# Attention memory into a feed-forward layer: eight small products side by side for scores and folds, heads ordered by even and odd, and three of the small accumulators moved to the first product's banks

## The chip, the core and the metric

The program runs on one core of one Trainium2 chip. A core has TensorE (matrix products, written to the accumulator memory PSUM, which has eight banks of 2 KB for each of its 128 partitions), VectorE (DVE in the profile), ScalarE (ACT), GpSimd (POOL) and SyncE (SP, which only issues DMAs here). The profile shows TensorE in two rows: PE, the products, and PEld, the loading of the stationary operand. The metric is the device time of one execution in microseconds (us).

## The reference

For each of 8 batches and 8 heads there are 576 tokens, a head width of 64 and 32 memory slots. What is computed, cut to what matters:

```python
a = exp(phi - max(phi, tokens)); a = a / sum(a, tokens)      # (b, h, s, 32)
k_m, v_m = a.T @ k, a.T @ v                                  # (b, h, 32, 64)
scores = q @ k_m.T / 8;  attn = softmax(scores, slots)       # (b, h, s, 32)
x = attn @ v_m                                               # tokens x 512
h = x @ w_in;  g = h * cos(h);  out = g @ w_out              # 512 -> 2048 -> 512
```

There are 4608 tokens in all. The inputs are float32, the two weights float64.

## The kernel before, in words

The product `attn @ v_m @ w_in` is regrouped: for each batch the 8 x 32 memory slots are multiplied into `w_in` once (the "fold", 256 x 2048), and the tokens are then multiplied with the folded weight. So the first large product has a contraction of 256 (two chunks of 128, index g) in place of 512.

**The main loop** (from line 660) has 192 steps: 12 groups of 384 tokens by 16 slices of the inner width. A step takes the first product of its slice (`gemm1`, line 493, into one of three banks of the pool ps_h), the cosine (`act`, `act_end`, lines 502 to 519: ACT, two DVE operations, ACT, DVE, ACT, DVE, after the fifth of which the bank is free), and the second product of a slice some five steps earlier (`gemm2`, line 537, into three banks of the pool ps_acc). From the second group on, float16 parts take the place of float32: a step has six products of 384 columns (or twelve of 192, where a group spans two batches) and nine of 512. A pair of batches takes 48 steps.

**The preparation of a batch** (`prep`, a generator: `memory`, line 214, then `attend`, line 324) is threaded into the steps before its first use. The job list (line 645) gives each batch its stretch of steps; the loop advances the generator so that it would reach 24 resumptions at the end of the stretch (NSTEP, lines 641 and 688). In order the resumptions hold: the maximum of phi spread over the partitions ("top", a product with the identity for the first four batches; a GpSimd reduction, `maximum`, line 204, from the fifth on); subtraction and Exp; the memory sums psA, one token chunk of 128 for each resumption, five in all, the last of 64 tokens (line 247: eight products of 32 columns a chunk, four side by side in the four 32-column strips); the loads of the next batch and the division (X, line 261); the transposition tpx (line 267) into km and vm (lines 274 to 277), which are zeroed first and hold a pair of heads as a block-diagonal 128 x 64; a bound on v for its scale (lines 281 to 287); the scores in three blocks of 256, 256 and 64 tokens (line 349: four products of 128 rows by 64 columns, two side by side, into one bank, then one DVE transposition, line 351); then the softmax and its split into two float16 parts.

**The fold** (lines 421 to 445) is placed by a second list (line 649): for each batch four quarters of the inner width (index q), two halves each (index g), a half every second step. From the third batch on a half is eight products in `fold_psum`: the high part vp of v_m against four strips, then its low part vl, which is padded with zeros in the rows of the other part of `w_in`, against the same four strips. Each product takes 128 rows, 32 columns and 512 columns of weights (line 432). ACT and DVE then split the bank into two float16 parts (lines 438 and 439).

**Banks.** Three pools share the eight banks: ps_acc has three, ps_h three (lines 51 and 52), and ps_s two (line 53), from which top, psA, tpx, each block of scores and each half of a fold take one.

**Order.** The kernel's framework gives each engine a fixed order of instructions when the program is built. It starts from the order of the code, but puts later work ahead of an instruction whose bank or operand its own estimates call not ready; only instructions that are pinned (`tc.keep_in_program_order`) stay. At run time each engine works through its own list, with semaphores for the rest.

## Time and profile before

| | |
|---|---|
| median of 3 runs | 719.82 us (718.49 to 720.54) |
| the profiled execution | 718.65 us, of which its span is 716.6 us |
| mean granted TensorE clock | 0.990 |
| PE busy | 694.8 us, 97% of the span |
| DVE busy | 570.0 us, 80% |
| ACT busy | 520.8 us, 73% |
| POOL busy | 14.1 us, 2% |

A row of the timeline has the start, the time from the first start to the last end, the engine, the line, the operation, the tiles (out<-in), the shapes and the count. Products overlap: one of 512 columns shows 0.38 us, but the next one starts 0.216 us after it. A float32 product is two rows, one for each of its passes. "128\*32" is the part of the array that a product takes: rows by columns.

### The profile page before, as it was taken

Reading aid. Unit: us, or ns where it says so; the run is one execution under the profiler, and the core shown is the slowest. Engines: PE = TensorE matmul, PEld = TensorE weight load, DVE = VectorE, ACT = ScalarE, POOL = GpSimd, SP = SyncE. Lnnn points to the kernel's source line nnn. Section 1 sums busy time; section 2 is a strip of 40 time slices with the busy share of each in tenths; the row PEclk is TensorE's granted clock in tenths of the full one; section 3 lists DMA queues with packets and bytes.
Section 4 is the critical chain, followed back from the end, with each engine's and each line's share of the span. In section 5 each row is a group of like instructions: output and inputs, shape, how many; then the busy total and the mean of one; then the engine's idle time right before and its main releaser. Section 6 shows DMA issues by size and latency. Waiting matters only on the chain.

```text
span 716.6 us, 12018 instructions
## 1 busy us (share of the span) xinstructions
PE 694.8 (97%) x4578; PEld 357.2 (50%) x4578; DVE 570.0 (80%) x1256; ACT 520.8 (73%) x965; POOL 14.1 (2%) x34
## 2 busy tenths in 40 slices
PE   7689999999999999999999999999999999999997
PEld 3244444565454445565444544666444544555553
DVE  2868999998988997679877997679776987676753
ACT  1789999899886875668757685678767785665653
POOL 0000000000000000000000100000000000000000
PEclk9799999999999999999999999999999999999999
DMA  8995881426405300152103310152100000100101
GB/s 291 381 330 168 310 291 42 121 60 188 149 7 161 111 1 1 45 167 67 45 1 123 107 49 1 45 167 68 44 1 1 22 24 1 45 1 1 45 0 45
DMA packets 31561, 66.78 MB, mean 93 GB/s; under 512 B 2192, under 2 KB 11024, under 8 KB 31504
## 3 DMA queue, kind: packets, MB, share of 16 engines
q1 hardware_dynamic: 27184, 58.15, 25.1%
q10 hardware_dynamic: 4320, 7.87, 2.9%
q8 instruction: 36, 0.59, 0.3%
q14 instruction: 21, 0.17, 0.1%
HBM read 52.38 MB, written 9.44 MB: 86 GB/s over the span
## 4 chain that ended last, share of the span: by engine, by line
PE 60%; ACT 17%; DVE 16%; DMA 4%; issue 2%; SPq 1%; POOL 0%; ACTq 0%; DVEq 0%
PE acc L537 34%; PE hp L493 18%; PE pv L432 3%; ACT u L512 2%; DVE u L516 2%; DMA phi<-in_phi 2%; DVE u L508 2%; DVE gp L519 2%; ACT u L502 2%; ACT L512 2%; DVE gp L507 1%; DMA kv<-in_kv 1%; PE sc L349 1%; ACT L237 1%; PE psA L247 1%
## 5 line engine op out<-in xcount | busy, mean ns | idle before, releaser
L537 PE MATMUL acc<-wo,gp 128*128 128x512 f16 x1584 | 371.2, 379 | 0.0
L537 PEld LDWEIGHTS <-gp 128*128 128x128 f16 x1584 | 153.4, 98 | 161.5 <-issue 2.6
L493 PE MATMUL hp<-aT,vw 128*128 128x192 f16 (+1 forms) x1440 | 202.6, 284 | 0.8 <-DVE u L516 0.4
L493 PEld LDWEIGHTS <-vw 128*128 128x128 f16 x1440 | 125.1, 98 | 82.3 <-issue 30.0
L512 ACT ACTIVATE u<-u 128x384 f32<-128x384 f32 x192 | 99.7, 522 | 86.6 <-DVE u L508 85.7
L516 DVE SCALAR_TENSOR_TENSOR u<-hp,u 128x384 f32<-128x384 f32 x176 | 96.8, 552 | 45.7 <-ACT u L512 43.4
L502 ACT ACTIVATE u<-hp,cu 128x192 f32<-128x192 f32 (+1 forms) x240 | 110.3, 491 | 18.2 <-PE hp L493 11.8
L519 DVE TENSOR_TENSOR gp<-u,gp 128x384 f16<-128x384 f32 x176 | 96.6, 551 | 29.9 <-ACT gp L518 29.3
L518 ACT CAST gp<-u 128x384 f16<-128x384 f32 x176 | 89.0, 509 | 38.7 <-DVE u L516 36.7
L508 DVE TENSOR_TENSOR u<-u,gp 128x384 f32<-128x384 f32 x192 | 105.7, 552 | 3.2
L507 DVE CAST gp<-u 128x384 int32<-128x384 f32 x192 | 67.4, 353 | 20.6 <-ACT u L502 18.9
L532 PE MATMUL acc<-wo,gp 128*128 128x512 f32 x96 | 45.5, 603 | 1.6 <-DVE gp L514 1.6
L439 DVE SCALAR_TENSOR_TENSOR vw<-pv,vw 128x512 f16<-128x512 f32 x48 | 33.0, 689 | 5.1 <-ACT vw L438 3.8
L438 ACT ACTIVATE vw<-pv 128x512 f16<-128x512 f32 x48 | 28.3, 590 | 7.4 <-PE pv L432 6.5
L484 PE MATMUL hp<-aT,vf 128*128 128x384 f32 x64 | 26.4, 546 | 4.2 <-DVE gp L514 2.0
L512 ACT ACT_TABLE_LOAD x23 | 29.5, 1283 | 0.4
L532 PEld LDWEIGHTS acc<-wo,gp 128*128 128x128 f32 x96 | 17.0, 190 | 20.7 <-issue 14.9
L247 PE MATMUL psA<-kv,phi 128*32 128x129 f32 (+1 forms) x640 | 23.5, 276 | 2.8 <-DMA kv<-in_kv 1.5
L553 ACT ACTIVATE ob<-acc,os 128x512 f32<-128x512 f32 x28 | 18.5, 682 | 8.1 <-PE acc L537 5.2
L247 PEld LDWEIGHTS psA<-kv,phi 128*32 128x32 f32 (+1 forms) x640 | 16.1, 109 | 13.3 <-issue 6.9
L484 PEld LDWEIGHTS hp<-aT,vf 128*128 128x128 f32 x64 | 12.5, 207 | 17.7 <-DVE gp L514 4.6
L349 PE MATMUL sc<-q,km 128*64 128x256 f32 (+3 forms) x192 | 20.6, 343 | 0.0
(126 smaller groups left out, 549.5 us busy)
## 6 DMA issues: line engine op xcount, KB each, us to landing
kv<-in_kv SPq DMA_DIRECT2D x32, 516.0 KB, 5.8
q<-in_qT SPq DMA_DIRECT2D x8, 1152.0 KB, 6.4
raw_out<-in_w_out SPq DMA_DIRECT2D x8, 1024.0 KB, 5.0
out<-ob ACTq DMA_DIRECT2D x30, 256.0 KB, 2.1
raw_in<-in_w_in SPq DMA_DIRECT2D x6, 1024.0 KB, 8.4
phi<-in_phi SPq DMA_DIRECT2D x8, 512.0 KB, 7.2
w_in_sb<-w_in_parts SPq DMA_DIRECT2D x12, 256.0 KB, 4.1
phiT<-in_phiT SPq DMA_DIRECT2D x4, 576.0 KB, 6.4
```

Source lines behind the costliest of these rows:

```text
L247: nc.tensor.matmul(psA[32 * j:32 * (j + 1), g * KV:(g + 1) * KV], lhsT=a[:n, c, h * M:(h + 1) * M], rhs=kvs[c][:n, h * KV:(h + 1) * KV], s ...
L484: nc.tensor.matmul(hp[:, :GT], lhsT=st["vf", q][:, g, fo * P:(fo + 1) * P], rhs=st["aTf"][:, g], start=(g == 0), stop=(g == 1))
L493: nc.tensor.matmul(hp[:, c0:c0 + n], lhsT=vw[:, wi, g, fo * P:(fo + 1) * P], rhs=aT[:, ai, g, c1:c1 + n], start=(k == 0), stop=(k == 5))
L502: ins = nc.scalar.activation(u[:, c0:c0 + n], hp[:, c0:c0 + n], AF.Copy, scale=st["cu", b] if grp else 1.0 / (2.0 * math.pi), bias=0.25)
L507: nc.vector.tensor_copy(out=ni, in_=u)
L508: nc.vector.tensor_tensor(out=u, in0=u, in1=ni, op=ALU.subtract)
L512: nc.scalar.activation(u, u, AF.Sin, scale=TWO_PI_BELOW)
L516: nc.vector.scalar_tensor_tensor(out=u, in0=hp[:, :GT], scalar=2.0 ** -17, in1=u, op0=ALU.mult, op1=ALU.mult)
L518: nc.scalar.copy(gp[:, 0], u)
L519: nc.vector.tensor_tensor(out=gp[:, 1], in0=u, in1=gp[:, 0], op=ALU.subtract)
L532: nc.tensor.matmul(accs[grp][t], lhsT=gp[:, t * P:(t + 1) * P], rhs=wo[:, f + 1], start=(f == 0), stop=(f == NF - 1))
L537: nc.tensor.matmul(accs[grp][t], lhsT=gp[:, gi, t * P:(t + 1) * P], rhs=parts[:, wi], start=(f == 0 and gi == 0 and wi == 0), stop=(f == N ...
```

## The change

For the third batch and those behind it (b >= 2; the first two stay as they are):

- The host puts the even heads ahead of the odd ones, and lays k ahead of v for the even, v ahead of k for the odd. After the transposition, k of the even heads and v of the odd stand in partitions 0 to 63, k of the odd and v of the even in partitions 64 to 127, without zeros between. km, vm and vl lose their padding, and GpSimd's two memsets and the mask of the bound on v fall away.
- A block of scores is eight products of 64 rows by 32 columns in place of four of 128 by 64. The even heads go to one bank, the odd to another, and each bank has a transposition of its own.
- A quarter of a fold is taken at once, into two banks: eight products of 128 by 32 with the high part, then eight of 64 by 32 with the low part. The call for the second half does nothing.
- top, psA and tpx take their bank from ps_h. The pool ps_s is left to scores and folds, which take both of its banks at a time.
- The five chunks of psA are issued without a resumption between them; the generator has four resumptions less, and what stands behind psA comes up to three steps earlier.

```diff
--- before.py
+++ after.py
@@ -58,6 +58,12 @@
     ident = const.tile([P, P], F32, name="ident")
     nc.sync.dma_start(out=ident, in_=eye)
 
+    HALF = (slice(0, D), slice(D, P))
     vmask = const.tile([P, 2, 2], F32, name="vmask")
     nc.vector.memset(vmask, 0.0)
     for j in range(4):
@@ -70,8 +76,11 @@
     def wo_parts(f):
         return wo[:, f].bitcast(F16).rearrange("p (w e) -> p w e", w=2)
 
-    vl = const.tile([P, NP, 2, M], F16, name="vl")
-    nc.vector.memset(vl, 0.0)
+    vl = const.tile([P, NP, M], F16, name="vl")
+    def one_ps(b, name):
+        return small_ps(name) if b < 2 else ps_h.tile([P, 512], F32, tag="ps_h", name=name)
 
     loads, st = {}, {}
 
@@ -217,7 +226,7 @@
 
             nmx = wk.tile([P, 2], F32, tag="nmx", name=f"nmx_{b}", bufs=1)
             nc.vector.tensor_reduce(out=nmx, in_=loads.pop(("phiT", b)), op=ALU.max, axis=AX.X)
-            top = small_ps(f"top_{b}")[:, 0:HM]
+            top = one_ps(b, f"top_{b}")[:, 0:HM]
             for g in range(2):
                 nc.tensor.matmul(top[:, g * P:(g + 1) * P], lhsT=nmx[:, g:g + 1].broadcast_to([P, P]), rhs=ident,
                                  start=True, stop=True)
@@ -239,7 +248,7 @@
         if b:
             yield
         kvs = loads.pop(("kv", b))
-        psA = small_ps(f"psA_{b}")
+        psA = one_ps(b, f"psA_{b}")
         for c, (s0, n) in enumerate(TCH):
             for g in range(2):
                 for j in range(4):
@@ -248,7 +257,8 @@
                         psA[32 * j:32 * (j + 1), g * KV:(g + 1) * KV],
                         lhsT=a[:n, c, h * M:(h + 1) * M], rhs=kvs[c][:n, h * KV:(h + 1) * KV],
                         start=(c == 0 and g == 0), stop=(c == 4), skip_group_check=True)
-            yield
+            if b < 2 or c == 4:
+                yield
         if b >= 1 and b + 1 < B and b + 1 != 2:
             load_phi(b + 1)
             load_kv(b + 1)
@@ -262,25 +272,39 @@
                                     op0=ALU.mult)
         if b:
             yield
-        tpx = small_ps(f"tpx_{b}")
+        tpx = one_ps(b, f"tpx_{b}")
         for g in range(2):
             nc.tensor.matmul(tpx[:, g * P:(g + 1) * P], lhsT=X[:, g], rhs=ident, start=True, stop=True)
-        km = wk.tile([P, NP, 2 * M], F32, tag="km", name=f"km_{b}", bufs=1)
-        vm = wk.tile([P, NP, 2 * M], F32, tag="vm", name=f"vm_{b}")
-        nc.gpsimd.memset(km, 0.0)
-        nc.gpsimd.memset(vm, 0.0)
-        tv = tpx[:, 0:HM].rearrange("p (c t m) -> p c t m", t=2, m=M)
-        lo, hi = slice(0, D), slice(D, P)
-        nc.scalar.mul(km[lo, :, 0:M], tv[lo, :, 0], 1.0 / math.sqrt(D))
-        nc.scalar.mul(km[hi, :, M:2 * M], tv[hi, :, 1], 1.0 / math.sqrt(D))
-        nc.vector.tensor_copy(out=vm[hi, :, 0:M], in_=tv[hi, :, 0])
-        nc.vector.tensor_copy(out=vm[lo, :, M:2 * M], in_=tv[lo, :, 1])
+        n = 2 * M if b < 2 else M
+        km = wk.tile([P, NP, n], F32, tag="km", name=f"km_{b}", bufs=1)
+        vm = wk.tile([P, NP, n], F32, tag="vm", name=f"vm_{b}")
+        if b < 2:
+            nc.gpsimd.memset(km, 0.0)
+            nc.gpsimd.memset(vm, 0.0)
+        lo, hi = HALF
+        if b < 2:
+            tv = tpx[:, 0:HM].rearrange("p (c t m) -> p c t m", t=2, m=M)
+            nc.scalar.mul(km[lo, :, 0:M], tv[lo, :, 0], 1.0 / math.sqrt(D))
+            nc.scalar.mul(km[hi, :, M:2 * M], tv[hi, :, 1], 1.0 / math.sqrt(D))
+            nc.vector.tensor_copy(out=vm[hi, :, 0:M], in_=tv[hi, :, 0])
+            nc.vector.tensor_copy(out=vm[lo, :, M:2 * M], in_=tv[lo, :, 1])
+        else:
+            tv = tpx[:, 0:HM].rearrange("p (g j m) -> p g j m", g=2, m=M)
+            for g in range(2):
+                nc.scalar.mul(km[HALF[g]], tv[HALF[g], g], 1.0 / math.sqrt(D))
+                nc.vector.tensor_copy(out=vm[HALF[1 - g]], in_=tv[HALF[1 - g], g])
         st["km", b], st["vm", b] = km, vm
         yield
-        l1 = wk.tile([P, 4], F32, tag="l1", name=f"l1_{b}")
-        nc.vector.tensor_reduce(out=l1, in_=X.rearrange("p g (t d) -> p (g t) d", t=2), op=ALU.add, axis=AX.X,
-                                apply_absolute_value=True)
-        nc.vector.tensor_tensor(out=l1, in0=l1, in1=vmask.rearrange("p g t -> p (g t)"), op=ALU.mult)
+        if b < 2:
+            l1 = wk.tile([P, 4], F32, tag="l1", name=f"l1_{b}")
+            nc.vector.tensor_reduce(out=l1, in_=X.rearrange("p g (t d) -> p (g t) d", t=2), op=ALU.add, axis=AX.X,
+                                    apply_absolute_value=True)
+            nc.vector.tensor_tensor(out=l1, in0=l1, in1=vmask.rearrange("p g t -> p (g t)"), op=ALU.mult)
+        else:
+            l1 = wk.tile([P, 2], F32, tag="l1", name=f"l1_{b}")
+            nc.vector.tensor_reduce(out=l1, in_=X.rearrange("p g x -> p (g x)")[:, D:3 * D].rearrange(
+                "p (t d) -> p t d", t=2), op=ALU.add, axis=AX.X, apply_absolute_value=True)
         l2 = wk.tile([P, 1], F32, tag="l2", name=f"l2_{b}")
         nc.vector.tensor_reduce(out=l2, in_=l1, op=ALU.max, axis=AX.X)
         l3 = wk.tile([P, 1], F32, tag="l3", name=f"l3_{b}")
@@ -312,10 +336,10 @@
             vp = wk.tile([P, NP, 2, M], F16, tag="vp", name=f"vp_{b}", bufs=1)
             for o in range(2):
                 here, there = slice(o * D, (o + 1) * D), slice((1 - o) * D, (2 - o) * D)
-                vm = st["vm", b][here, :, (1 - o) * M:(2 - o) * M]
+                vm = st["vm", b][here]
                 nc.scalar.activation(vp[here, :, o], vm, AF.Copy, scale=sv[here])
                 nc.scalar.activation(vp[there, :, o], vm, AF.Copy, scale=sv[here])
-                nc.vector.scalar_tensor_tensor(out=vl[here, :, o], in0=vm, scalar=sv[here], in1=vp[here, :, o],
+                nc.vector.scalar_tensor_tensor(out=vl[here], in0=vm, scalar=sv[here], in1=vp[here, :, o],
                                                op0=ALU.mult, op1=ALU.subtract)
             st["vp", b] = vp
 
@@ -343,6 +367,15 @@
 
         def scores(i):
             t0, n = BL[i]
+            if b >= 2:
+                sc = [small_ps(f"sc_{b}_{t0}_{g}") for g in range(2)]
+                for j in range(4):
+                    for g in range(2):
+                        nc.tensor.matmul(sc[g][M * j:M * (j + 1), :n], lhsT=km[HALF[g], j],
+                                         rhs=qt[HALF[g], j, t0:t0 + n], start=True, stop=True)
+                for g in range(2):
+                    nc.vector.transpose(at[:, 2 * t0 + g * n:2 * t0 + (g + 1) * n], sc[g][:, :n])
+                return
             sc = small_ps(f"sc_{b}_{t0}")
             for g in range(2):
                 for p in range(2):
@@ -418,19 +451,25 @@
         yield
 
 
-    def fold_psum(b, q, g):
-        pv = small_ps(f"pv_{b}_{q}_{g}")
+    def fold_32(q, g):
+        pv = small_ps(f"pv_1_{q}_{g}")
         for i in range(2):
             c = 2 * g + i
-            if b < 2:
-                nc.tensor.matmul(pv[D * i:D * (i + 1)], lhsT=st["vm", b][:, c],
-                                 rhs=w_in_sb[:, c, q * FS:(q + 1) * FS], start=True, stop=True)
-        if b >= 2:
-            for first in (True, False):
-                for j in range(4):
-                    c, o = 2 * g + j // 2, 1 - j % 2
-                    nc.tensor.matmul(pv[M * j:M * (j + 1)], lhsT=(st["vp", b] if first else vl)[:, c, o],
-                                     rhs=st["w2", q][:, c, o], start=first, stop=not first, skip_group_check=True)
+            nc.tensor.matmul(pv[D * i:D * (i + 1)], lhsT=st["vm", 1][:, c], rhs=w_in_sb[:, c, q * FS:(q + 1) * FS],
+                             start=True, stop=True)
+        return pv
+    def fold_16(b, q):
+        pv, w2 = [small_ps(f"pv_{b}_{q}_{g}") for g in range(2)], st["w2", q]
+        for g in range(2):
+            for j in range(4):
+                nc.tensor.matmul(pv[g][M * j:M * (j + 1)], lhsT=st["vp", b][:, j, 1 - g], rhs=w2[:, j, 1 - g],
+                                 start=True, stop=False, skip_group_check=True)
+        for j in range(4):
+            for g in range(2):
+                v = HALF[1 - g]
+                nc.tensor.matmul(pv[g][M * j:M * (j + 1)], lhsT=vl[v, j], rhs=w2[v, j, 1 - g],
+                                 start=False, stop=True, skip_group_check=True)
         return pv
 
     def split_fold(b, vw, g, src):
@@ -442,7 +481,11 @@
     def fold(b, q, g):
         if g == 0:
             st["vw", b, q] = wk.tile([P, 2, 2, FS], F16, tag="vw", name=f"vw_{b}_{q}", bufs=8)
-        split_fold(b, st["vw", b, q], g, fold_psum(b, q, g))
+        if b == 1:
+            split_fold(b, st["vw", b, q], g, fold_32(q, g))
+        elif g == 0:
+            for x, pv in enumerate(fold_16(b, q)):
+                split_fold(b, st["vw", b, q], x, pv)
 
     def fold_first(j):
         q, r = divmod(j, 2)
@@ -711,10 +754,16 @@
 
     q, k, v, phi = (np.asarray(inputs[n]) for n in ("q", "k", "v", "phi"))
     w_in, w_out = np.asarray(inputs["moe_w_in"]), np.asarray(inputs["moe_w_out"])
+    k, v, phi = k.copy(), v.copy(), phi.copy()
+    order = list(range(0, H, 2)) + list(range(1, H, 2))
+    for a in (k, v, phi):
+        a[2:] = a[2:, order]
     kv = np.ones((B, S, H, KV), k.dtype)
     kt, vt = k.transpose(0, 2, 1, 3), v.transpose(0, 2, 1, 3)
-    kv[:, :, 0::2, 0:D], kv[:, :, 0::2, D:2 * D] = kt[:, :, 0::2], vt[:, :, 0::2]
-    kv[:, :, 1::2, 0:D], kv[:, :, 1::2, D:2 * D] = vt[:, :, 1::2], kt[:, :, 1::2]
+    for bs, even, odd in ((slice(0, 2), slice(0, H, 2), slice(1, H, 2)), (slice(2, B), slice(0, 4), slice(4, H))):
+        kv[bs, :, even, 0:D], kv[bs, :, even, D:2 * D] = kt[bs, :, even], vt[bs, :, even]
+        kv[bs, :, odd, 0:D], kv[bs, :, odd, D:2 * D] = vt[bs, :, odd], kt[bs, :, odd]
     laid = {
         "phi": np.ascontiguousarray(phi.transpose(0, 2, 1, 3)).reshape(B, S, HM),
         "phiT": np.ascontiguousarray(phi[:NT].transpose(0, 1, 3, 2)).reshape(NT, HM, S),
```

## The prediction

> **What bounds the kernel now.** I read the page first, then the busy time by stretches, the waits of PE, and the chain that ended last; then single visits of PE to the small products.
>
> ```profile
> span 716.6 us, 12018 instructions
> PE 694.8 (97%) x4578; PEld 357.2 (50%) x4578; DVE 570.0 (80%) x1256; ACT 520.8 (73%) x965; POOL 14.1 (2%) x34
> ```
>
> The page says PE, but 97% is an average. The stretches and the waits of PE behind 218 us say where it is true:
>
> ```profile
> 160.00:218.00 58.00, 57.23 (x427) 29.85 (x426) 49.80 (x115) 51.10 (x87) 0.97 (x3) 1.00 0.40 123
> 218.00:640.00 422.00, 420.67 (x2983) 217.84 (x2983) 340.44 (x771) 298.69 (x582) 9.54 (x16) 1.00 0.16 53
> ```
>
> ```profile
> PE pv L432 <- ACT vp L317: 0.4, 1, 0.4
> PE psA L247 <- ACT phi L237: 0.4, 2, 0.2
> PE hp L493 <- DVE u L516: 0.3, 1, 0.3
> ```
>
> The columns of the first are the stretch, its length, and the busy time of PE, PEld, DVE, ACT and POOL, then the granted clock (1.00) and DMA. From 218 to 640 us, where five of the six changed batches have their scores and nearly all of their folds, PE is busy 420.7 of 422 us and waits 1.1 us in all. Time taken off PE there should come off the end. There are two exceptions. Before 218 us, in the preparation of the third batch, DVE (49.8 of 58) and ACT (51.1) are as full as PE, and the chain runs over them. And the chain leaves PE twice later, for some 42 us each (302 to 344, and alike 465 to 507):
>
> ```profile
> 310.50 7.29 DMA phi<-in_phi
> 317.82 0.69 DVE mx L207
> ...
> 343.58 0.48 DVE u L516
> ```
>
> There PE has work, but the work of DVE and ACT is just as late: PE's lists are full only because second products are put ahead while banks of the first are missing. What PE saves in those two stretches counts only if that chain gets shorter too.
>
> **The folds.** A visit to one half of a fold, with the products of 512 columns ahead and those of the next step behind:
>
> ```profile
> 373.94 2.11 PE L537 MATMUL acc<-wo,gp 128*128 128x512 f16 x9
> 375.98 0.40 PE L432 MATMUL pv<-w_in_sb,vp 128*32 128x512 f16 x4
> 376.20 0.39 PE L432 MATMUL pv<-w_in_sb,vl 128*32 128x512 f16 x4
> 376.52 1.15 PE L493 MATMUL hp<-aT,vw 128*128 128x384 f16 x6
> ```
>
> Nine products of 0.216 us bring 373.94 to 375.88; the fold starts 0.10 later, its second round 0.22 after the first, and the next product 0.32 after that, which is a round and 0.10 more. So the visit costs 376.52 - 373.94 - 1.94 = 0.64 us: two rounds of four products side by side, and a switch of the array's shape of 0.10 on each side. There are 48 such visits, 30.7 us; seven lie directly beside psA or scores (one is seen below, at 383.15) and share a switch, 0.2 each, so 29.3 us.
>
> What a switch inside a visit costs is seen in psA, whose last chunk has 64 rows. Two chunks of one shape, and then two of which the second is the one of 64 rows (this view runs them together):
>
> ```profile
> 211.88 0.81 PE L537 MATMUL acc<-wo,gp 128*128 128x512 f16 x3
> 212.62 1.09 PE L247 MATMUL psA<-kv,phi 128*32 128x129 f32 x32
> 213.65 0.82 PE L493 MATMUL hp<-aT,vw 128*128 128x384 f16 x4
> ```
>
> ```profile
> 308.65 0.59 PE L537 MATMUL acc<-wo,gp 128*128 128x512 f16 x2
> 309.18 1.22 PE L247 MATMUL psA<-kv,phi 128*32 128x129 f32 x32
> 310.33 0.50 PE L493 MATMUL hp<-aT,vw 128*128 128x192 f16 x4
> ```
>
> The first visit costs 213.65 - 211.88 - 0.65 = 1.12 us, the second 310.33 - 308.65 - 0.43 = 1.25, so the inner switch is 0.13.
>
> After the change a quarter is one visit: switch 0.10, two rounds for the high parts 0.44, inner switch 0.13, the low parts, and 0.10. If the eight products of 64 by 32 run side by side they are one round, 0.22: together 0.99 us, where two halves cost 1.28. Twenty-four quarters cost 23.8 us; the saving is 5.5 us. No row shows two products in different halves of the rows at once, so this has two bounds: one round or two. I take one, since strips beside each other do run at once (four products in 0.40 us), and the two halves write different banks.
>
> **The scores.** A block of 256 and a block of 64 tokens:
>
> ```profile
> 319.80 0.59 PE L537 MATMUL acc<-wo,gp 128*128 128x512 f16 x2
> 320.33 1.08 PE L349 MATMUL sc<-q,km 128*64 128x256 f32 x8
> 321.35 1.16 PE L493 MATMUL hp<-aT,vw 128*128 128x192 f16 x12
> ```
>
> ```profile
> 327.26 1.24 PE L537 MATMUL acc<-wo,gp 128*128 128x512 f16 x5
> 328.44 0.45 PE L349 MATMUL sc<-q,km 128*64 128x64 f32 x8
> 328.82 0.59 PE L493 MATMUL hp<-aT,vw 128*128 128x192 f16 x5
> ```
>
> The first costs 321.35 - 319.80 - 0.43 = 1.12 us (eight rows, two at a time: four rounds of 0.216, and switches), the second 328.82 - 327.26 - 1.08 = 0.48. A batch costs 2.72, six 16.3, less 0.8 where two blocks share a visit: 15.5 us. Eight at a time leave two of the four rounds: 1.12 - 0.43 = 0.69, and for the small block half of its 0.28 between the switches, so 0.34. Six batches cost 10.3 us; the saving is 5.2. The same doubt holds as for the folds.
>
> **The memory sums.** psA keeps its products, but its five chunks become one visit. Today they lie in two to four:
>
> ```profile
> 380.64 1.46 PE L537 MATMUL acc<-wo,gp 128*128 128x512 f16 x6
> 382.03 0.65 PE L247 MATMUL psA<-kv,phi 128*32 128x129 f32 x16
> 382.61 0.60 PE L537 MATMUL acc<-wo,gp 128*128 128x512 f16 x2
> 383.15 0.40 PE L432 MATMUL pv<-w_in_sb,vp 128*32 128x512 f16 x4
> 383.37 0.39 PE L432 MATMUL pv<-w_in_sb,vl 128*32 128x512 f16 x4
> 383.59 0.61 PE L247 MATMUL psA<-kv,phi 128*32 128x129 f32 x16
> ```
>
> One chunk alone costs 382.61 - 380.64 - 1.30 = 0.67, a further one 1.12 - 0.67 = 0.45. A batch in three visits costs 0.67 + 1.12 + 1.25 = 3.04; six, as they lie, 18.1 us. One visit is 1.25 + 3 x 0.45 = 2.6, six 15.6: a saving of 2.5 us. PE then stands for 2.6 us at one stretch without a first product; DVE and ACT have at that point several slices of cosine to work off, so it costs nothing, unless they have not, where it costs at most those 2.6 us for a batch.
>
> **Other engines and the loads.** DVE's rows:
>
> ```profile
> L351 DVE STREAM_TRANSPOSE at<-sc 128x512 f32<-128x512 f32 x15 | 10.6, 707 | 0.9 <-PE sc L349 0.9
> L372 DVE STREAM_TRANSPOSE aT<-at 128x256 f32<-128x256 f32 x2 | 0.8, 424 | 0.0
> L351 DVE STREAM_TRANSPOSE at<-sc 128x128 f32<-128x128 f32 x7 | 2.1, 305 | 0.0
> L439 DVE SCALAR_TENSOR_TENSOR vw<-pv,vw 128x512 f16<-128x512 f32 x48 | 33.0, 689 | 5.1 <-ACT vw L438 3.8
> ```
>
> A block's transposition of 0.71 us becomes two of 0.42, that of the small block (0.31) two of at most 0.31: 0.6 us more a batch at most, less the mask and half of the reduction that fall away. DVE has 82 us to spare from 218 to 640, so it is off the path except in the two stretches above. GpSimd's memsets go; nobody waited for them. The loads of the next batch's phi, kv and q move with the generator, up to three steps ahead, in SP's queue; only loads stand behind them there. phi has one buffer, so its load starts when psA has been read through. With psA in one visit this comes sooner, which helps the 7.29 us of the chain above.
>
> **New waits.** Each of the 24 quarters and 18 blocks needs both banks of ps_s at once, where today one is filled while the other is read. From below this costs nothing: the order puts other products between. From above it costs the full reading time, two DVE passes: 2 x 0.42 = 0.84 us for a block, 2 x 0.69 = 1.38 for a quarter, 48 us in all. I take 1.0 us in all, near the lower end, since PE's present waits for banks (0.3) show that the planned order fits the chip. top, psA and tpx now hold one of the three banks of the first product: between nothing and the 2.6 us above for a batch; I take 0.5 in all.
>
> **Sum.** PE saves 5.5 + 5.2 + 2.5 = 13.2 us. Off it come the third batch's scores and memory sums and part of the fourth's sums, before 218 us (1.6), half of what the fifth and seventh batches save in the two stretches that DVE and ACT set (2.2, so 1.1), and the new waits (1.5). That leaves 9.0: 718.65 - 9.0 = 709.6 us for an execution like the profiled one. The median of the runs shown is 1.2 above it; I add a part of that: **710.0 us**.
>
> **The rivals.**
>
> *Row halves do not run side by side* (the change then doesn't do what it says). A quarter costs 0.99 + 0.22 = 1.21, twenty-four 29.0: 0.3 saved. Scores cost 16.3 in separate visits: 0.8 lost. psA's 2.5 stay. With the losses of the sum PE gains about 1: 717.5 us, no difference that can be told (0.3%, or 2.2 us, is about what a measurement of this kernel can tell from none). Against it speaks only what strips do. The Trainium skill, TensorEngine Tiling (Array Packing), under Tiling Modes, lists 64 by 32 as eight independent tiles that load and multiply in parallel. By that rule the savings of 5.5 and 5.2 stand; no row here shows such a pair. Chance 0.11.
>
> *DVE and ACT become the bound in the preparations.* DVE is 81% busy from 218 to 640, and the attention parts now lie in fewer, faster steps, with two halves of a fold (1.38 us of DVE) falling in one step of about 2.9 us. Then what is saved inside the preparations is lost, and only the folds outside them count: about two thirds of 5.5, and 1 of psA, 4.5 in all: 714 us. For it speak the two stretches; against it that DVE recovers between them. The Trainium skill, same page, under Performance Considerations (PSUM Bottleneck), warns that tiling speeds up TensorE but not the reading of PSUM. The trace bears this out only in the stretches named. Chance 0.14.
>
> *Slower: PE stands before the two banks of ps_s.* A block of scores that follows a quarter or another block must wait until DVE has read both banks; in the sixth and eighth batches the step lists put a quarter and a block in one step and two blocks in the next. If all 18 blocks wait 0.84 and a quarter of the folds' reading (0.25 of 1.38 for 24) shows as well, that is 15 + 8 = 23 us, less 10.5 saved: 731 us. It decides from 0.27 us a user (42 of them, 11.2 us: the saving and 0.3%). Against it speaks that PE's list has second products ready at nearly every point. Chance 0.09.
>
> **How the numbers follow.** The forecast has 0.66. With the second rival a gain has 0.80, no difference 0.11, slower 0.09. The range reaches from 703.5, where all 13.2 us count and the chain shortens a little, to 717.5, into the first rival; what lies outside is the last rival, half of the first, and little below.
>
> **What would show it.** In the changed profile a quarter should show eight low products within one span of about 0.40 us, starting a few ns apart, and cost 0.99; a block of 256 should cost 0.69; psA should be one visit of about 2.6 with its bank from ps_h. Low products in two rounds mean the first rival; PE rows of waiting for DVE at scores or folds above 5 us in all the third; waits of hp for DVE at line 516's bank, or a chain that stays on DVE behind 218 us, the second. The prediction is wrong if visits cost what I say and the end doesn't move, or if they don't.

## The result, and the profile after

The changed kernel takes 730.2 us (median of 4 runs, 729.72 to 730.93); the kernel before, on the same chip, 719.4 (718.49 to 720.54). The ratio is 1.0158 [1.014 to 1.0177]: slower by 1.6%, where a gain was forecast. The profiled execution took 729.72 us, its span 727.9.

From the page of the changed kernel, the busy times and the shares of the chain that ended last:

```profile
PE 692.0 (95%) x4722; PEld 355.8 (49%) x4722; DVE 570.4 (78%) x1267; ACT 515.0 (71%) x963; POOL 9.7 (1%) x22
PE 47%; DVE 23%; ACT 21%; DMA 5%; issue 2%; SPq 1%; ACTq 0%; DVEq 0%
```

The stretch from 218 to 640 us, with the columns as before (PE, PEld, DVE, ACT, POOL, clock, DMA), and what PE waited for behind 160 us (in all, times, longest):

```profile
218.00:640.00 422.00, 409.29 (x2980) 210.78 (x2977) 329.38 (x755) 286.69 (x562) 6.65 (x9) 0.99 0.16 54
```

```profile
PE hp L536 <- DVE u L559: 3.8, 8, 0.9
PE acc L580 <- ACT ob L596: 3.6, 4, 2.0
PE sc L374 <- ACT km L294: 2.9, 3, 1.4
PE sc L374 <- DVE vw L478: 2.3, 2, 1.4
```

In the stretch where PE had been idle for 1.3 us (422 - 420.67) it is now for 12.7. DVE and ACT hold 44% of the chain, where they held 33% before. None of these four waits had been of any size: the longest total in the kernel before is 0.4 us.

**The visits themselves came out as forecast.** A quarter of a fold, a block of 256 scores and a psA, each with the products ahead and behind:

```profile
287.99 2.11 PE L580 MATMUL acc<-wo,gp 128*128 128x512 f16 x9
290.02 0.61 PE L466 MATMUL pv<-w_in_sb,vp 128*32 128x512 f16 x8
290.57 0.41 PE L471 MATMUL pv<-w_in_sb,vl 64*32 64x512 f16 x8
290.91 1.17 PE L536 MATMUL hp<-aT,vw 128*128 128x192 f16 x12
```

```profile
220.78 2.11 PE L580 MATMUL acc<-wo,gp 128*128 128x512 f16 x9
222.81 0.66 PE L374 MATMUL sc<-q,km 64*32 64x256 f32 x16
223.41 1.15 PE L536 MATMUL hp<-aT,vw 128*128 128x384 f16 x6
```

```profile
305.81 2.33 PE L580 MATMUL acc<-wo,gp 128*128 128x512 f16 x10
308.07 2.54 PE L256 MATMUL psA<-kv,phi 128*32 128x129 f32 x80
310.55 2.15 PE L536 MATMUL hp<-aT,vw 128*128 128x192 f16 x24
```

Worked out as in the prediction they cost 290.91 - 287.99 - 1.94 = 0.98 us (forecast 0.99), 223.41 - 220.78 - 1.94 = 0.69 (0.69) and 310.55 - 305.81 - 2.16 = 2.58 (2.6). The eight low products lie within 0.41 us: the two halves of the rows do work side by side.

**But most blocks of scores are not one visit.** The eighth batch, where halves of blocks come one by one:

```profile
569.58 0.34 PE L536 MATMUL hp<-aT,vw 128*128 128x384 f16 x1
569.84 0.64 PE L374 MATMUL sc<-q,km 64*32 64x256 f32 x8
570.41 0.34 PE L536 MATMUL hp<-aT,vw 128*128 128x384 f16 x1
570.68 0.64 PE L374 MATMUL sc<-q,km 64*32 64x256 f32 x8
```

A half shows x8: four products in two passes. It costs 570.41 - 569.58 - 0.16 = 0.67 us, as much as the whole block of x16 (0.69), since eight products side by side take the time of four. A split block so costs 1.34, more than the 1.12 of the old form. Eleven of the 18 blocks are split, because the order puts other work between: 28 visits behind 160 us where there were 15. Eight of them are split as here, one bank at a time. The other three, the first blocks of the third, fifth and seventh batches, are split after one product, and not for a bank. The fifth batch, PE and then ACT:

```profile
316.30 0.62 PE L374 MATMUL sc<-q,km 64*32 64x256 f32 x2 [1.39 <-ACT km L294]
318.76 1.10 PE L374 MATMUL sc<-q,km 64*32 64x256 f32 x14
```

```profile
318.44 0.27 ACT L294 ACTIVATE km<-tpx 64x128 f32<-64x128 f32 x1
```

ACT writes km in two parts, of the even and of the odd heads. The second part ends at 318.71, and only then can the first product for the odd heads start.

**Where the time went, as a sum.** PE's records from 160 us to the end, for both profiled executions: the interval from each product's start to the next, less the step of the main products (0.216, 0.1625 and 0.0825 us for 512, 384 and 192 columns), put down to the visit that it belongs to, or, where the next product starts late by over 0.04 us (0.095 more ahead of a visit), to a wait.

| us behind 160 us | before | after | difference | forecast |
|---|---|---|---|---|
| visits to folds | 30.8 | 24.6 | -6.1 | -5.5 |
| visits to scores | 15.4 | 17.8 | +2.4 | -5.2 |
| visits to psA | 17.6 | 15.5 | -2.1 | -2.5 |
| waits ahead of scores | 0.0 | 6.8 | +6.8 | |
| waits ahead of acc | 0.0 | 4.5 | +4.5 | |
| waits ahead of hp | 1.6 | 5.4 | +3.8 | |
| waits ahead of top, psA, tpx, folds | 2.0 | 2.7 | +0.7 | |
| all waits | 3.6 | 19.4 | +15.8 | +1.5 |
| main products at the halved clock | 0.0 | 2.9 | +2.9 | |

With -1.5 for work that lies on the other side of the cut, this is the 11.3 us by which the span grew.

**What such a wait looks like.** The sixth batch, PE and then DVE: a quarter of a fold, and a block of scores behind it in the same step.

```profile
398.66 0.41 PE L471 MATMUL pv<-w_in_sb,vl 64*32 64x512 f16 x8
399.00 1.15 PE L536 MATMUL hp<-aT,vw 128*128 128x384 f16 x6
399.99 0.59 PE L580 MATMUL acc<-wo,gp 128*128 128x512 f16 x2
402.03 0.64 PE L374 MATMUL sc<-q,km 64*32 64x256 f32 x8 [1.45 <-DVE vw L478]
402.60 0.82 PE L580 MATMUL acc<-wo,gp 128*128 128x512 f16 x3
403.35 0.88 PE L374 MATMUL sc<-q,km 64*32 64x256 f32 x8
```

```profile
400.58 0.80 DVE L562 TENSOR_TENSOR gp<-u,gp 128x384 f16<-128x384 f32 x1
401.30 0.68 DVE L478 SCALAR_TENSOR_TENSOR vw<-pv,vw 128x512 f16<-128x512 f32 x1
401.90 0.54 DVE L562 TENSOR_TENSOR gp<-u,gp 128x384 f16<-128x384 f32 x1
402.37 0.68 DVE L478 SCALAR_TENSOR_TENSOR vw<-pv,vw 128x512 f16<-128x512 f32 x1
```

The quarter's products end at 399.07. DVE, with cosines ahead of it in its list, reads the first bank until 401.98, and PE stands until 402.03, with the second products of 402.60 behind the block in its list. The second bank is read until 403.05, so the block's other half is a visit of its own at 403.35. At this place both costs, the wait and the split, come from one thing: two banks that are wanted together and read late. It is not the only cause: of the waits ahead of scores the profile puts 2.5 us down to readers of the two banks (2.3 for vw, 0.2 for a transposition) and 2.9 to km.

The group's end in the fourth batch, PE and ACT, looks alike:

```profile
293.86 1.15 PE L536 MATMUL hp<-aT,vw 128*128 128x192 f16 x12
297.01 0.81 PE L580 MATMUL acc<-wo,gp 128*128 128x512 f16 x3 [2.00 <-ACT ob L596]
```

```profile
294.66 0.58 ACT L477 ACTIVATE vw<-pv 128x512 f16<-128x512 f32 x1
295.37 0.51 ACT L561 CAST gp<-u 128x384 f16<-128x384 f32 x1
295.79 0.59 ACT L477 ACTIVATE vw<-pv 128x512 f16<-128x512 f32 x1
296.28 0.68 ACT L596 ACTIVATE ob<-acc,os 128x512 f32<-128x512 f32 x1
```

The quarter's two readings lie ahead of the reading that frees the accumulator of the finished group (ob), and PE stands 2.00 us. That they cause this wait is not shown, and late_quarters below speaks against it.

**The clock.** Three of these waits (2.00 us here, 1.45 in the sixth batch, 1.39 for km at 316.30) are followed by a stretch at half the granted clock. Below is the stretch with the wait of 2.00 us, and then the three at half the clock (the third number from the end is the clock, 1.00 or 0.50):

```profile
294.40:297.80 3.40, 1.40 (x11) 0.75 (x9) 2.32 (x4) 2.79 (x6) 0.00 (x0) 1.00 0.00 0
297.80:301.20 3.40, 3.05 (x9) 1.11 (x8) 1.26 (x4) 2.53 (x7) 0.00 (x0) 0.50 0.60 231
318.30:321.70 3.40, 3.40 (x30) 1.99 (x27) 3.33 (x9) 2.60 (x8) 0.00 (x0) 0.50 0.10 29
403.60:407.00 3.40, 3.40 (x28) 0.67 (x20) 2.30 (x9) 2.63 (x6) 0.00 (x0) 0.50 0.00 0
```

Each costs at most half of 3.4, so 1.7 us, at most 5 us together; the table shows 2.9 of it, and the visits inside (403.35 above) hold some of the rest. The kernel before has none between its start and its last microsecond.

### The profile page after: what moved, and what is told of

Same layout as the page of the kernel before. It is cut to its first block, busy times and chain, and to the rows that moved or that the text cites. A ratio compares the mean times of both kernels' runs of the same rounds, so it can differ in the third digit from the quotient of the medians.

```text
span 727.9 us, 12289 instructions
## 1 busy us (share of the span) xinstructions
PE 692.0 (95%) x4722; PEld 355.8 (49%) x4722; DVE 570.4 (78%) x1267; ACT 515.0 (71%) x963; POOL 9.7 (1%) x22
## 4 chain that ended last, share of the span: by engine, by line
PE 47%; DVE 23%; ACT 21%; DMA 5%; issue 2%; SPq 1%; ACTq 0%; DVEq 0%
PE acc L580 28%; PE hp L536 13%; DVE u L551 4%; DVE u L559 4%; ACT u L555 4%; DVE gp L562 3%; DMA phi<-in_phi 3%; ACT u L545 3%; ACT gp L561 2%; DVE gp L550 2%; DVE vw L478 2%; PE psA L256 2%; PE sc L374 1%; DMA kv<-in_kv 1%; ACT L555 1%
## 5 line engine op out<-in xcount | busy, mean ns | idle before, releaser
L536 PEld LDWEIGHTS <-vw 128*128 128x128 f16 x1440 | 128.2, 98 | 80.4 <-issue 22.5
L545 ACT ACTIVATE u<-hp,cu 128x192 f32<-128x192 f32 (+1 forms) x240 | 111.1, 492 | 29.7 <-PE hp L536 24.4
L478 DVE SCALAR_TENSOR_TENSOR vw<-pv,vw 128x512 f16<-128x512 f32 x48 | 31.4, 683 | 3.0 <-ACT vw L477 3.0
L575 PEld LDWEIGHTS acc<-wo,gp 128*128 128x128 f32 x96 | 17.1, 190 | 20.5 <-issue 14.7
L477 ACT ACTIVATE vw<-pv 128x512 f16<-128x512 f32 x48 | 26.5, 587 | 0.3 <-PE pv L471 0.2
L256 PE MATMUL psA<-kv,phi 128*32 128x129 f32 (+1 forms) x640 | 21.1, 275 | 2.9 <-DMA kv<-in_kv 1.4
L374 PE MATMUL sc<-q,km 64*32 64x256 f32 (+1 forms) x288 | 16.9, 363 | 5.8 <-ACT km L294 2.9
L527 PEld LDWEIGHTS hp<-aT,vf 128*128 128x128 f32 x64 | 12.2, 203 | 17.6 <-DVE gp L557 4.6
```

What stands on the lines that cost most here:

```text
L256: nc.tensor.matmul(psA[32 * j:32 * (j + 1), g * KV:(g + 1) * KV], lhsT=a[:n, c, h * M:(h + 1) * M], rhs=kvs[c][:n, h * KV:(h + 1) * KV], s ...
L478: nc.vector.scalar_tensor_tensor(out=vw[:, 1, g], in0=src, scalar=T, in1=vw[:, 0, g], op0=ALU.mult, op1=ALU.subtract)
L536: nc.tensor.matmul(hp[:, c0:c0 + n], lhsT=vw[:, wi, g, fo * P:(fo + 1) * P], rhs=aT[:, ai, g, c1:c1 + n], start=(k == 0), stop=(k == 5))
L545: ins = nc.scalar.activation(u[:, c0:c0 + n], hp[:, c0:c0 + n], AF.Copy, scale=st["cu", b] if grp else 1.0 / (2.0 * math.pi), bias=0.25)
L575: nc.tensor.matmul(accs[grp][t], lhsT=gp[:, t * P:(t + 1) * P], rhs=wo[:, f + 1], start=(f == 0), stop=(f == NF - 1))
```

## The experiments

The theory: PE's time counts, as forecast, but the waits for the two paired banks, at places where the steps put a quarter and a block together, and for a later ACT and DVE eat it. Its rivals: PE's time does not set the end at all; one part (the banks in ps_h, or the resumptions that are left out) does the harm and the products are innocent; the new order of the heads costs something by itself. This table has every kernel, by the same sum as above (behind 160 us; the span is the whole profiled execution's); the ratios are of the medians of each job, with their intervals.

| kernel | span | visits | waits | halved clock | ratio |
|---|---|---|---|---|---|
| before | 716.6 | 63.7 | 3.6 | 0 | 1 |
| after | 727.9 | 57.9 | 19.4 | 2.9 | 1.0158 [1.014, 1.0177] |
| layout_only | 719.2 | 63.7 | 6.1 | 0 | 1.0025 [1.0007, 1.0044] |
| scores_only | 722.5 | 63.0 | 8.0 | 1.7 | 1.0063 [1.0041, 1.0085] |
| folds_only | 719.7 | 59.8 | 11.3 | 0 | 1.0031 [1.0009, 1.0053] |
| products_only | 725.0 | 58.2 | 16.8 | 1.5 | 1.0107 [1.0082, 1.0132] |
| banks_only | 728.9 | 63.1 | 15.6 | 1.3 | 1.0165 [1.0132, 1.0197] |
| yields_kept | 726.6 | 56.0 | 21.4 | 0 | 1.0108 [1.0086, 1.013] |
| small_banks | 723.0 | 57.6 | 16.9 | 0 | 1.0098 [1.0077, 1.0119] |
| padded | 730.1 | 62.2 | 16.9 | 1.6 | 1.0186 [1.0161, 1.0211] |
| no_low | 707.6 | 53.1 | 5.7 | 0 | 0.9885 [0.9861, 0.9909] |
| stretched | 720.8 | 54.3 | 18.4 | 0 | 1.0061 [1.0041, 1.0082] |
| late_quarters | 736.3 | 59.3 | 24.4 | 3.2 | 1.0261 [1.0231, 1.029] |
| both_lists | 724.3 | 55.0 | 20.0 | 0.8 | 1.009 [1.007, 1.0111] |
| fewer_steps | 717.7 | 61.2 | 7.0 | 0 | 1.0014 [0.9996, 1.0033] |
| moved_banks | 726.6 | 64.7 | 10.8 | 0 | 1.0104 [1.0071, 1.0138] |
| banks_stretched | 714.8 | 61.0 | 5.9 | 0 | 0.9984 [0.9969, 1.0] |
| readers_first | 716.5 | 53.7 | 14.7 | 0 | 1.0008 [0.9992, 1.0024] |
| ob_first | 717.4 | 53.7 | 15.3 | 0 | 1.0 [0.9987, 1.0013] |
| before_readers | 720.9 | 63.3 | 7.7 | 0 | 1.0028 [1.0015, 1.0042] |

### Does PE's time count at all?

```diff
-            for first in (True, False):
+            for first in (True,):
...
-   rhs=st["w2", q][:, c, o], start=first, stop=not first, skip_group_check=True)
+   rhs=st["w2", q][:, c, o], start=True, stop=True)
```

> The kernel before without the four low-part products of each half fold (the output then lacks the low float16 part of v): 48 rounds of 0.216 us, 10.4 us less work for PE, and nothing else taken away. If PE's own time sets the end, as the prediction had it, 708 to 711 us. If the fixed order and DVE and ACT are as tight as PE, and time freed on PE turns into waits, 715 to 722 us.

It takes 711.25 us against 719.02, 7.8 less, just above the first range. The visits got 10.6 us shorter, waits took 2.1 back. In the kernel before PE's time does set the end; the rival that it does not is out, and the prediction's reading of the stretches was right.

### One part at a time

Four edits undo the parts of the changed kernel. Edit a puts psA's resumptions back, edit b the banks, edit c the scores (four products of 128 by 32 for each half, with a padded km, into one bank), edit d the halves of the folds (vl padded, one bank, one half at a time).

```diff
@@ edit a @@
-            if b < 2 or c == 4:
-                yield
+            yield
@@ edit b @@
-        return small_ps(name) if b < 2 else ps_h.tile([P, 512], F32, tag="ps_h", name=name)
+        return small_ps(name)
@@ edit c @@
-                sc = [small_ps(f"sc_{b}_{t0}_{g}") for g in range(2)]
+                sc = small_ps(f"sc_{b}_{t0}")
...
+                        nc.tensor.matmul(sc[M * j:M * (j + 1), g * n:(g + 1) * n], lhsT=km[:, g, j],
+                                         rhs=qt[:, j, t0:t0 + n], start=True, stop=True)
+                nc.vector.transpose(at[:, 2 * t0:2 * (t0 + n)], sc[:, :2 * n])
@@ edit d @@
-        elif g == 0:
-            for x, pv in enumerate(fold_16(b, q)):
-                split_fold(b, st["vw", b, q], x, pv)
+        else:
+            split_fold(b, st["vw", b, q], g, fold_16(b, q, g))
```

All four, so that only the order of the heads and the unpadded v are left (layout_only):

> The new order of heads and the unpadded v, but the products as before: scores as 128x32 products with zero padding into one bank, folds in halves with the padded low part, the three small accumulators in ps_s and all resumptions kept. Every theory expects the time of before, 719.4 us within 2; more than that either way would say that the fixed order of instructions alone, which is planned anew for each program, moves the time by as much.

Edits a, b and d, which leaves the scores (scores_only):

> Only the scores are 64x32 products in two banks. Theory A (waits for the pair of banks eat the gain): scores' products fall by up to 5 us, but PE waits for banks or km and visits split, 719 to 725 us. Theory B (the waits come from the dropped resumptions and the moved accumulators, not from the products): the gain stands, 714 to 716 us.

Edits a, b and c, which leaves the folds (folds_only):

> Only the folds are taken by quarters with 64x32 low products in two banks; scores are padded 128x32 products in one bank. Theory A: the folds' 6.1 us stand mostly, 713 to 716 us, but the two waits of the second product for the accumulators (2.0 and 0.9 us, both behind a quarter at the start of a group) return, with a halved clock behind them. Theory B: 712 to 714 us and no such wait.

Edits a and b (products_only):

> Both kinds of 64x32 products, but the small accumulators in ps_s and all resumptions kept. Theory A (each part brings its own waits, and they add): 723 to 728 us. Theory B (accumulators and resumptions bring the loss): 712 to 720 us.

Edits c and d, which leaves the banks and the resumptions (banks_only):

> Products as before (one bank each), but the small accumulators in ps_h and four resumptions less. Theory A: psA's 2 us are saved and nothing lost, 716 to 719 us. Theory B: the preparation runs earlier and the first product has a bank less, so PE waits 5 to 12 us, 724 to 731 us.

Edit a alone (yields_kept), and edit b alone (small_banks):

> The changed kernel with its four resumptions back, so that scores and softmax stand at their old steps; accumulators in ps_h. Theory A (the two banks and the moved accumulators bring the waits): 725 to 731 us. Theory B (the earlier steps bring them): 714 to 721 us.

> The changed kernel with top, psA and tpx back in ps_s, four resumptions less. If the first product's missing bank brings the waits: 714 to 721 us. If the earlier steps or the pair of banks bring them: 726 to 733 us.

The new order costs 0.25%, hardly to be told. Neither kind of product alone makes the kernel faster. folds_only saves 3.8 us of visits and pays 7.7 of waits; it is level with layout_only (721.44 against 720.91 us) and above both of its ranges. scores_only saves almost nothing, since some of its blocks are split too and others take their two banks one after the other, and pays 4.4 of waits and a halved clock. Banks and resumptions alone, with products of the old cost, lose as much as the whole change. Undoing the resumptions or the banks in the changed kernel gives back 2.6 and 3.7 us, not 11. So no single part is to blame, and the losses do not add up: products_only (7.7) and banks_only (11.8) would make 19.5 us. The longest wait of banks_only is of another kind, seen on PE and DVE:

```profile
189.77 4.70 PE L574 MATMUL acc<-wo,gp 128*128 128x512 f16 x21
197.56 1.76 PE L530 MATMUL hp<-aT,vw 128*128 128x384 f16 x5 [3.10 <-DVE u L553]
```

```profile
195.76 0.69 DVE L411 SCALAR_TENSOR_TENSOR aT<-back,aT 128x512 f16<-128x512 f32 x1
196.36 0.71 DVE L408 STREAM_TRANSPOSE back<-at 128x512 f32<-128x512 f32 x1
196.99 1.45 DVE L553 SCALAR_TENSOR_TENSOR u<-hp,u 128x384 f32<-128x384 f32 x3
```

The generator is ahead of its old place, and the third batch's softmax lies in DVE's list ahead of the operation that frees a bank of ps_h (line 553). PE has no bank and stands for 3.10 us.

### Is it the form of the products?

Zeros in place of the missing rows: 128 by 32 products with two banks, all else as changed.

```diff
-   lhsT=km[HALF[g], j], rhs=qt[HALF[g], j, t0:t0 + n]
+   lhsT=km[:, g, j], rhs=qt[:, j, t0:t0 + n]
-   lhsT=vl[v, j], rhs=w2[v, j, 1 - g]
+   lhsT=vl[:, j, 1 - g], rhs=w2[:, j, 1 - g]
```

> The changed kernel with every 64x32 product made a zero-padded 128x32 one: same banks, same resumptions, and about 11 us more work for PE (two rounds more for each block of 256 tokens, one more for each quarter). Theory A (PE's own time still sets the end, plus waits): 738 to 742 us. Theory B (in the changed kernel the fixed order and the other engines set the end, and PE only waits in it): 728 to 734 us, PE's waits shrinking by what its products grow.

It is 2 us slower than the change in the span, and its visits are only 4.3 longer. The larger figure that I expected was wrong: without the 64 by 32 form a quarter has no inner switch any more, and a split block has its cost already. Its 732.65 us lie in the range of theory B, but its waits (16.9 against 19.4) fell by 2.5 us only, so it settles nothing on them. It shows that the form itself does no harm.

### The steps in which a quarter and a block meet

Two changes of the lists: the generator spread over its stretch anew (20 resumptions in place of 24), which parts a quarter and a block; or the last two quarters of the fourth, sixth and eighth batches two steps later, away from the end of a group; or both.

```diff
stretched
-   want = math.ceil((i - s + 1) * NSTEP / (e - s + 1))
+   want = math.ceil((i - s + 1) * (NSTEP if b < 2 else 20) / (e - s + 1))
late_quarters
-   folds.setdefault(use - before + 4 * q + 2 * g, []).append((b, q, g))
+   folds.setdefault(use - before + 4 * q + 2 * g + 2 * (b > 2 and b % 2 and q >= 2), []).append((b, q, g))
```

> The changed kernel, its generator advanced so that 20 resumptions (the number that is left) fill the batch's stretch: scores and softmax at about their old steps, no quarter in one step with a block of scores, psA still one visit. If the collisions of the lists bring the loss: 720 to 724 us. If the replanned order brings waits wherever the work stands: 725 to 731 us.

> The changed kernel, the last two quarters of the fourth, sixth and eighth batches two steps later, so that ACT no longer has two splits of a quarter ahead of the reading of a group's accumulators: the waits of the second product for ACT (3.6 us) and one halved clock (1.7 us) should go, 725 to 727 us; 729 to 731 if they only move.

> Both changes of the lists in the changed kernel. If each removes the waits that it is meant for: 715 to 720 us. If the order planned anew finds other waits: 724 to 730 us.

Spreading the generator gives 7 of the 11 us back: the halved clock is gone and scores fall from 17.8 to 14.2 us. Later quarters, from which I expected a gain as well, make it worse by about 8, outside both of their ranges; the two together (both_lists) lie between, at 726.16 us. What PE waited for most in late_quarters:

```profile
PE sc L374 <- ACT km L294: 5.3, 2, 2.7
PE acc L580 <- ACT ob L596: 4.7, 5, 2.5
```

The two waits for km are those of the changed kernel, in the fifth and the seventh batch, which were 1.39 and 1.31 us there. The wait at the group's end in the fourth batch is still there too:

```profile
298.10 0.81 PE L580 MATMUL acc<-wo,gp 128*128 128x512 f16 x3 [2.51 <-ACT ob L596]
```

It is 2.51 us in place of 2.00, though the quarter now lies behind it (its products start at 300.64) and ACT has only the cosine ahead of ob. So the quarter's readings are not what makes this wait; what does stays open. Where the steps lie is worth 7 us one way and 8 the other, as much as the changed products were to bring. That the meeting of a quarter and a block is by itself the cost is not shown: stretched, which parts them, also moves all other work of the preparation, and late_quarters does not part them (in the sixth batch the block still waits 1.43 us behind its quarter).

### The kernel before with the other parts of the change

The products stay those of before; only the resumptions (fewer_steps), only the banks (moved_banks; top and tpx are changed like psA in the diff), or both with 20 resumptions spread as in stretched (banks_stretched).

```diff
fewer_steps
-            yield
+            if b < 2 or c == 4:
+                yield
moved_banks
-        psA = small_ps(f"psA_{b}")
+        psA = one_ps(b, f"psA_{b}")
```

> The kernel before with the four resumptions of psA dropped and nothing else: five chunks in one visit, scores and softmax up to three steps earlier. If the earlier steps bring the loss of 11 us that moved accumulators and dropped resumptions have together: 726 to 730 us. If the moved accumulators bring it: 716 to 720 us.

> The kernel before with top, psA and tpx of the third batch and those behind it in ps_h, all resumptions kept. If the first product's missing bank brings the loss: 724 to 730 us, psA being held over four steps. If the earlier steps bring it: 718 to 721 us.

> The kernel before with moved accumulators, psA in one visit, and 20 resumptions spread over the stretch. If only the steps matter: 715 to 719 us, psA's 2 us saved. If the missing bank matters: 722 to 730 us.

The resumptions alone change nothing that can be told. The banks alone cost 7.5 us; psA holds one of the three banks of the first product for four steps, and behind it tpx and hp wait for DVE to free another. In moved_banks:

```profile
322.12 0.71 PE L270 MATMUL tpx<-ident,X 128*128 128x128 f32 x4 [0.56 <-DVE u L519]
325.13 1.07 PE L496 MATMUL hp<-aT,vw 128*128 128x192 f16 x11 [1.00 <-DVE u L519]
```

psA in one visit does not mend this alone (banks_only has it). With psA in one visit and the steps spread the banks do no harm: 0.9984, with an interval that ends at 1.0. It is the only kernel with all of the reference's work whose interval does not reach above the kernel before, and no more than that can be said.

### Who reads the two banks late?

If the readers stand too late in the lists of DVE and ACT, putting them ahead should give the rest back. On top of stretched, with the framework's priority for the reading of folds, scores and tpx (km and vm, alike, left out of the diff); then also for the reading of a finished group (ob); and as a control the same priority in the kernel before.

```diff
readers_first
             for x, pv in enumerate(fold_16(b, q)):
-                split_fold(b, st["vw", b, q], x, pv)
+                with tc.high_priority():
+                    split_fold(b, st["vw", b, q], x, pv)
...
-                    nc.vector.transpose(at[:, 2 * t0 + g * n:2 * t0 + (g + 1) * n], sc[g][:, :n])
+                    with tc.high_priority():
+                        nc.vector.transpose(at[:, 2 * t0 + g * n:2 * t0 + (g + 1) * n], sc[g][:, :n])
...
ob_first
-            nc.scalar.activation(ob, accs[grp][t], AF.Copy, scale=osc)
+            with tc.high_priority():
+                nc.scalar.activation(ob, accs[grp][t], AF.Copy, scale=osc)
```

> The changed kernel with 20 resumptions spread over the stretch, and the readers of the paired banks (the splits of a quarter, the transpositions of scores, km and vm) put at the head of the framework's order. If banks that are read late make PE wait: 713 to 719 us. If the readers are late because their inputs are, or the delay only moves to the first product's bank: 721 to 727 us.

> readers_first with ACT's reading of a finished group's accumulators put at the head of the order as well. In readers_first the second product still waits 3.0 us for it. If that goes and nothing takes its place: 714 to 717 us, faster than both kernels; if PE meets the next late bank instead: 718 to 720 us.

> A control: the kernel before, with the readers of its folds, scores and transpositions at the head of the order, and nothing else. PE waits for none of them there, so no change, 717 to 721 us; if the head of the order helps by itself, 712 to 716 us, and what readers_first won back is not a repair of the changed kernel.

readers_first is at 718.54 us, level with the kernel before and about 4 us below stretched (a ratio of 1.0008 against 1.0061). The sixth batch there, PE, and what PE still waited for:

```profile
397.53 2.11 PE L583 MATMUL acc<-wo,gp 128*128 128x512 f16 x9
399.57 0.66 PE L375 MATMUL sc<-q,km 64*32 64x256 f32 x16
400.16 1.15 PE L539 MATMUL hp<-aT,vw 128*128 128x384 f16 x6
```

```profile
PE hp L539 <- DVE u L562: 3.4, 6, 1.3
PE acc L583 <- ACT ob L599: 3.0, 7, 0.9
PE sc L375 <- DVE at L379: 1.7, 3, 0.7
```

The block is one visit of 0.69 without a wait. PE's visits are now 10.0 us shorter than before, of the 13.2 of the forecast, and waits are 11.2 longer: the saving is there on PE and is spent on waits in other places. Priority for ob as well (ob_first) does not take its wait away: the second product still waits 2.9 us for it (3.0 without), and all waits are 15.3 us in place of 14.7. The control gains nothing in the kernel before (1.0028), so the priority is no gain of its own; it repairs a part of what the change broke.

## Why the prediction was wrong

- **What bounds the kernel**: right. no_low shows that PE's time comes off the end, about 8 of 10 us.
- **The folds**: right. A quarter costs 0.98 against 0.99, all 24 save 6.1 us against 5.5. The first rival is out: the low products run side by side. The Trainium skill, TensorEngine Tiling (Array Packing), Tiling Modes, has 64 by 32 as eight independent tiles; the trace agrees, with eight products in 0.41 us.
- **The scores**: a whole block costs the 0.69 and a whole small one 0.37 (forecast 0.34), but eleven of 18 are split, and a half costs what the whole does. In place of -5.2 us stands +2.4. The prediction took it as given that the eight products stay together; eight blocks were split between the two banks, three because the second part of km came late.
- **The memory sums**: right (2.58 against 2.6; 2.1 us against 2.5). The 0.5 us for its bank was too little: the first product waits 3.8 us more in the changed kernel, and with the banks put back (small_banks) the kernel gains 3.7. The 7.5 us of moved_banks are no measure of it, since psA is held over four steps there. With psA in one visit and the steps spread the banks cost nothing (banks_stretched). That an earlier load of phi would help the chain did not come true: DVE still stands for it, 1.18 us ahead of 316.25 (1.02 ahead of 317.82 in the kernel before), and the operation that frees a bank of hp and, over ACT, the second part of km are held up behind it.
- **The step that failed** is in "New waits": "I take 1.0 us in all, near the lower end, since PE's present waits for banks (0.3) show that the planned order fits the chip", and 0.5 for the banks of ps_h: 1.5 us, where the waits came to 15.8 us more, with 2.9 us and more of halved clock behind them. The 0.3 belonged to the old program's order. The framework makes a new one for each program; layout_only, with the banks and nearly the products of before, already waits 2.5 us more. The term was also too narrow. At the two banks themselves the profile shows 2.5 us, far nearer the lower bound than the 48 of the upper; most of the rest lies ahead of hp (3.8), where it had 0.5, and at places that it put at nothing: the accumulators of the second product (4.5) and km (2.9).
- **The third rival** came true in part: PE stands for the two banks in the sixth batch, one of the two that it named, and in the fourth. Its sign, more than 5 us of waiting for DVE at scores or folds, did not appear (2.5 us). Its 731 us agrees with 730.2 by accident: it counted 23 us of waits for ps_s, where all waits ahead of scores are 6.8, and did not have the split blocks, the waits for km, ob and hp, or the clock.
- **The second rival**: one of its signs did appear, hp waiting for the DVE operation that frees its bank (3.8 us), and the chain did move towards DVE and ACT (44% from 33%). But they are not fuller: DVE is busy 329.4 of 422 us, where it was 340.4. In the rows shown, what frees a bank lies in DVE's list behind other work.

Shown by the runs: spreading the steps (7 us) and putting the readers first (about 4) together win back the 11 us between the two kernels. How much of each is owed to what the edit was meant for is not shown, since every edit also makes a new order, and layout_only (2.4 us) and late_quarters (8) show that a new order moves the time by such amounts. Not settled either: why the 11 us of waits that are left in readers_first stay. That the framework's estimates of time place PE's work too early for DVE and ACT would explain it, but no run here separates that from a true want of banks.

## What to carry to other kernels

Where an order is planned by a program, near-zero waits say little about the next program: cost every bank that a change makes two users share at once, and count a saving on the bounding engine only after asking which reader will be late. Products that run side by side pay only when all of their banks and operands are there together, since a part costs as much as the whole; if they must share, try the readers of these banks ahead. Before judging such a change, try it with the steps moved by one or two: here that alone was worth as much as the change.

## What the runs showed of the hardware

Waits of 1.39 to 2.00 us were followed by a stretch of 3.4 us at half the clock (from 297.8, 318.3 and 403.6); in the 3.4 us ahead of each, PE was idle for 2.00, 1.94 and 1.45 us in all. The length of a wait alone does not decide: in stretched waits of up to 1.6 us had no such stretch behind them, and the 2.51 us of late_quarters had none either. The Trainium skill, TensorE: Matmul & The Clock Gate, Part 1, describes a free-running window of 3413 ns after which the clock is set; the 3.4 us agree. That a wait shared by two such windows counts less in each would fit the 2.51 us, but is not tested here. The Trainium skill, same page, in the section Why this matters for your kernels, advises to avoid idle gaps above about 3 us; here the measurement decides, and gaps of 1.39 to 2.00 us were followed by stretches that cost up to 1.7 us each on top of them.
